# A decode step and its gradients on one core: the zero runs of two outputs lengthened by parking a softmax tile in DRAM, and a weight pass in whole row blocks

## The chip, the core and the metric

The kernel runs on 1 core of one Trainium2 chip. The metric is device time in microseconds of one execution, and a result is the median over several runs. A core has TensorE (PE, with its weight loads shown as PEld), VectorE (DVE), ScalarE (ACT), GpSimd (POOL) and SyncE (SP), which all work beside each other, and 16 DMA engines, which move data between DRAM and the core's on-chip memory. In this kernel SP issues nearly all transfers, in program order, on one queue.

## The reference, cut to what matters

Two layers, A (attention of one token over a sliding window of the cache) and B (a two-matrix MLP with the mish activation), are applied twice: A1, B2, A3, B4. Both rounds use the same weights. The result is the output and the gradients of it with respect to the input, both caches and all weights.

```python
def _A_ref(x, k_cache, v_cache, wq, wo):
    W = min(4096, max(256, Sk // 4))                 # 4096 of Sk = 32768
    q = heads(x @ wq)                                # 32 heads of 128, 4 key/value heads
    k = repeat(k_cache[:, :, Sk - W:, :], 8); v = repeat(v_cache[:, :, Sk - W:, :], 8)
    p = softmax((q @ k.T) * (Dh ** -0.5))
    return merge(p @ v) @ wo                         # wq: 1024 x 4096, wo: 4096 x 1024
def _B_ref(x, w1, b1, w2):
    h = x @ w1 + b1                                  # w1: 1024 x 3584, w2: 3584 x 1024
    return (h * tanh(softplus(h))) @ w2
def _f(x, ...):
    x = x + _A_ref(_layernorm(x), ...); x = x + _B_ref(_layernorm(x), ...)
    x = x + _A_ref(_layernorm(x), ...); x = x + _B_ref(_layernorm(x), ...)
    return x
out, vjp = jax.vjp(_f, ...); grads = vjp(grad_out)
```

All data is bf16. Only the last 4,096 of 32,768 cache rows take part, so 28,672 rows of each of the 4 heads of both cache gradients (out_2 and out_3) are zero: 58.7 MB of zeros, which the kernel writes from a zeroed tile.

## The kernel before, in words

One token is a matrix-vector problem, so the kernel is a long chain of small steps, and beside it the weights are read (several times, since they don't all fit), the zeros are written, and at the end the weight gradients, outer products of the kept vectors, are written out.

The chain in order: `attn_fwd` A1, `mlp_B2_fwd`, `attn_fwd` A3, `mlp_B4` (forward and backward of the last layer in one pass over w1), `ln_bwd`, `attn_bwd` A3, `mlp_B2_bwd`, `attn_bwd` A1, and a list of output jobs (`run_jobs`) that starts inside the last `attn_bwd` through `out_step`.

**Tiles.** Large tiles stay in fixed places for the whole kernel: `wq`, `wo`, `K`, `V` and `misc`. `misc` has 128 partitions x 4,096 bf16, cut into four quarters of 1,024 columns (2 KB): `sB` (0), `sA` (1), `zlo` (2), `sC` (3). `sC` holds the softmax rows p of A1 from the first attention to the last step; `sB` holds those of A3, `sA` the score gradients ds of A3. Before A3, the first two quarters (`misc[:, 0:2048]`) also serve as slot 0 of the ring `r2`. `zlo` is always zero; `zt` (quarters 1 and 2) is zero from the end of `mlp_B2_fwd` until A3's ds is written.

**Zeros.** `zero_jobs` holds 112 units, 14 per head and output; a unit is 2,048 columns on 128 partitions, 512 KB. `zeros(n)` issues n units on SP, up to four adjoining ones in one transfer. The source `zsrc` is a zeroed tile and its width: it is repeated over the destination by a broadcast, so the width sets the length of the contiguous run that one packet moves. The calls of `zeros` with their counts are written by hand into the stages. Until the end of `mlp_B2_fwd` the width is 1,024 columns (2 KB, `zlo`), then 2,048 (4 KB, `zt`) until the last block of B4's w1 pass, then 1,024 again, and from `out_step(0)` on 4,096 (8 KB, a part of `wo`).

**Weight loads.** `queue` is a list of loads in fixed order. `pump()` (L172) issues the first entries on SP as long as their slots are free; `rel(ring, i)` gives a slot back and pumps. The rings are `r2` (6 slots, w1 and w2 of the forward pass), `r4` (w1 blocks of B4), `rb` (w2 of the backward pass, slots of 2,048 columns of `K`) and `r8` (w1 of the backward pass, 8 slots of 1,792 columns of `K`). `r8` lies on the memory of `rb`: a slot of `rb` that no further w2 chunk needs becomes one or two slots of `r8` (L209). At the end the K heads are loaded again over `r8` (`K8`).

**The last w1 pass** (end of `mlp_B2_bwd`). w1's 8 row blocks of 128 rows are read as 16 halves of 128 x 1,792 (`w1h`). For each half TensorE turns 8 blocks, ACT copies them back over the half (`T8`, L235), VectorE does a multiply and sum over 768 columns (`ttr`, L593), and one half later `pairs` multiplies the turned blocks and releases the half's slot.

**Order.** The schedule is written by hand: SP works through its transfers in program order, and each waits for its data, its destination, and a free completion semaphore. SP uses eight of these in turn, so that in the trace a transfer is issued only once the one eight places earlier has landed.

Of the kernel before, what the change touches and what calls it, by code (L numbers as in the profile page):

```python
# [9 lines left out]
BF16 = mybir.dt.bfloat16  # L10
# [11 lines left out]
def kernel(  # L22
# [41 lines left out]
    ctx.enter_context(tc.manual_schedule())  # L64
    keep = ctx.enter_context(tc.tile_pool(name="keep", bufs=1))
    pt = ctx.enter_context(tc.tile_pool(name="pt", bufs=3, space=bass.MemoryType.PSUM))
    pone = ctx.enter_context(tc.tile_pool(name="pone", bufs=1, space=bass.MemoryType.PSUM))

    nc.scalar.preload_act_table_set("natural_log_exp_and_others")
# [14 lines left out]
    kp = kt([P, TJ, P], BF16, "kp")  # L84
    jk = kt([P, WC], BF16, "jk")
    misc = kt([P, 4096], BF16, "misc")
    sB, sA, zlo, zt, sC = misc[:, 0:1024], misc[:, 1024:2048], misc[:, 2048:3072], misc[:, 1024:3072], misc[:, 3072:4096]
    Kf = K[:].rearrange("p g t d -> p g (t d)")
    Kl = K[:].rearrange("p g t d -> p (g t d)")
    Vf = V[:].rearrange("p g t d -> p g (t d)")  # L90
# [47 lines left out]
    def zeros(n, after=None):  # L138
        while n > 0 and zero_jobs:
            zf, i = zero_jobs.pop(0)  # L140
            k = 1
            while k < min(n, 4) and zero_jobs and zero_jobs[0][1] == i + k:
                zero_jobs.pop(0)
                k += 1
            dst, run = zf[:, i * 2048:(i + k) * 2048], zsrc[1] if k * 2048 % zsrc[1] == 0 else 2048
            if run < k * 2048:
                d = nc.sync.dma_start(dst.rearrange("p (a b) -> p a b", b=run), zsrc[0][:, None, :].to_broadcast([P, k * 2048 // run, run]))
            else:
                d = nc.sync.dma_start(dst, zsrc[0][:, 0:run])
            gate(d, after)  # L150
            after = None
            n -= k
# [4 lines left out]
    slots = dict(r2=[misc[:, 0:2048]] + [wo[:, 20 + 2 * i:22 + 2 * i, :].rearrange("p h d -> p (h d)") for i in range(1, 6)],  # L157
                 r4=[Kl[:, 2048 * i:2048 * (i + 1)] for i in range(4, 8)])
    slots["rb"] = [Kl[:, 2048 * i:2048 * (i + 1)] for i in range(8)]
    slots["r8"] = [Kl[:, 2048 + F // 2 * i:2048 + F // 2 * (i + 1)] for i in range(8)]  # L160

    def w_view(w, key):
        if key[0] == "w2":
            return w.rearrange("p (t d) -> p t d", t=2), w2_v[key[1]]
        if key[0] == "w1h":
            t, hf = key[1] // 2, key[1] % 2
            w = w[:, 0:F // 2]
            return w, w1_v[:, t, hf * (F // 2):(hf + 1) * (F // 2)]
        b, i = key[1], key[2]
        nt = 2 if b < 3 else 4  # L170
        return w.rearrange("p (t f) -> p t f", t=nt), w1_v[:, nt * i:nt * i + nt, b * 1024:b * 1024 + 2048 // nt]

    def pump():
        while queue:
            it = queue[0]
            if it[0] == "w":
                fr = rings[it[1]]
                if not fr:
                    return
                i = fr.pop(0)  # L180
                v, src = w_view(slots[it[1]][i], it[2])
                nc.sync.dma_start(v, src)
                held[it[2]] = (v, it[1], i)
            elif it[0] == "K":
                fr = rings[it[1]]
                if len(fr) < 2:
                    return
                assert (fr.pop(0), fr.pop(0)) == (2 * it[2] - 4, 2 * it[2] - 3)
                nc.sync.dma_start(K[:, it[2], :, :], k_v[:, it[2]])
            elif it[0] == "K8":  # L190
                if rings["r8"][0:2 * it[1] + 2] != list(range(2 * it[1] + 2)):
                    return
# [12 lines left out]
            queue.pop(0)  # L205

    def rel(ring, i):
        if ring == "rb" and not any(it[0:2] == ("w", "rb") for it in queue):
            rings["r8"] += [6, 7] if i == 7 else [i - 1]  # L209
        else:  # L210
            rings[ring].append(i)
        pump()

    def take(key):
        return held.pop(key)
# [4 lines left out]
    queue += [("wo", s) for s in ([2, 3], [4, 5], [1])]  # L220
    queue += [("w", "r4", ("w1b", b, i)) for b in range(4) for i in range(4 if b < 3 else 2)]
    queue += [("K", "r4", g) for g in (3, 2)]
    queue += [("w", "rb", ("w2", c)) for c in range(NW2)] + [("w", "r8", ("w1h", i)) for i in range(16)]
    queue += [("K8", g) for g in range(G)]

# [232 lines left out]
    def attn_fwd(x_col, l, first, p_dst, F_, Z_):  # L459
        sv, n_bf, g0 = ln_fwd(x_col, l)  # L460
        if first:
            constants()
        zeros(Z_[0])
        big = two_banks()
        for t in range(TD):
            for n in range(8):
# [65 lines left out]
                    unit("V", Vf[:, g, u * 1024:(u + 1) * 1024])  # L532
        for h in range(2):
            nc.scalar.activation(p_dst[:, h * 512:(h + 1) * 512], big[h][:], ACT.Exp, bias=nb[:, 0:1], scale=-1.0)
        o_bf = opair[:, LI[l], :]
        go = nc.vector.tensor_copy(o_bf, acc[:])
        pps = sm_tile(P, HQ)
# [101 lines left out]
            nc.vector.tensor_mul(d3[:, 1, :], dps[:], m3[:, 1, :])  # L639

    def mlp_B2_fwd(x_col):
        zeros(4)
        sv, n_bf, g0 = ln_fwd(x_col, "B2")
        hacc = one_tile("acc", TF)
# [14 lines left out]
        mish(h, apair[:, 1, :], dact[:], TF, jkf)  # L659
        sv["dact"] = dact  # L660
        R, dps, ds = w2_pass(apair[:, 1, :], gpair[:, LI["B4"], :], {8: 1, 9: 1, 10: 1, 11: 1})
        nc.gpsimd.memset(sA, 0.0)
        make_identity(nc, ident_f)
        zsrc[:] = [zt, 2048]
        da4 = kt([P, TF], FP32, "da4")
        y = d_cols(R)
        x_new = kt([P, TD], FP32, "x_B2")
# [4 lines left out]
    def mlp_B4(x_col, da4):  # L672
# [64 lines left out]
        for b in range(4):  # L737
            fwd(b)
            fill(FB4[b][0])
            sel(b)  # L740
            act(b)
            turn(b, 0, 8 if b < 3 else 4)
            fill(FB4[b][1])
            bwd(b)
            if b == 3:
                zeros(2)
                zsrc[:] = [zlo, 1024]
            zeros(ZB4[b] - 2 * (b == 3))
        evac(jkf[:, 0:256], R[:, 0:256], 256, "D")
        dn = sm_tile(P, TD)  # L750
        for i in range(2):
# [68 lines left out]
    def mlp_B2_bwd(g_col, g_bf, sv, x3):  # L820
        bcast_g(g_bf)
        R, dps, ds = w2_pass(apair[:, 0, :], g_bf, {10: 1})
        zeros(3)
        dh = kt([P, TF], FP32, "dh_B2")
        da_merge(dh[:], dps, ds, sv["dact"][:])
        nc.vector.tensor_copy(hpair[:, 1, :], dh[:])
# [19 lines left out]
        def pairs(i, w, ring, sl):  # L846
            t, hf = i // 2, i % 2
            for k in range(8):
                fb = hf * NW2 + k
                mm(nacc[:, t:t + 1], w[:, k * P:(k + 1) * P], hpair[:, 1, fb:fb + 1], i == 0 and k == 0, hf == 1 and k == 7)  # L850
            rel(ring, sl)
            zeros({9: 2, 12: 1, 14: 1}.get(i, 0))

        for i in range(16):
            w, ring, sl = take(("w1h", i))
            T8([w[:, (k // 2) * 256 + k % 2:(k // 2) * 256 + k % 2 + 255:2] for k in range(8)], w[:, 0:1024], "A")
            ttr(w[:, 1024:1792], dhb[i % 2][:, 0:768], nv[:, i:i + 1])
            if pend:
                pairs(*pend.pop())
            pend.append((i, w, ring, sl))  # L860
# [311 lines left out]
```

## Time and profile before

| | |
|---|---|
| median of 3 runs | 426.61 us (425.5 to 426.96) |
| profiled execution, its own time | 426.93 us |
| its span, first to last instruction | 425.1 us |
| mean granted TensorE clock | 0.764 |
| TensorE, VectorE, ScalarE, GpSimd busy | 317.7, 234.5, 220.1, 13.8 us |
| DRAM read, written | 70.27 MB, 98.58 MB (397 GB/s over the span) |
| DMA packets | 43,990, 169.44 MB; 37,036 under 8 KB |

How to read it: times are microseconds. Line numbers (L182) are those of the kernel below; L142 to L149 are the zeros, L182 the weight loads from the rings, L204 other loads from `queue`, L966 to L1102 the outputs. "out<-in" names the tiles an instruction writes and reads. An arrow behind an idle time names what ended it. A stretch's DMA share is the time that packets started in it took, over 16 engines; it can be a little over 1, as packets overlap. A DMA's landing is the time at which its completion is signalled.

| from | to (about) | stage |
|---|---|---|
| 0 | 65 us | A1 forward: wq, K, V, wo loaded |
| 65 | 109 us | B2 forward: w1 and w2 in ring `r2` |
| 109 | 145 us | A3 forward |
| 145 | 218 us | B4 forward and backward, w1 in ring `r4` |
| 218 | 247 us | A3 backward |
| 247 | 292 us | B2 backward: w2 in `rb`, then w1 in `r8` |
| 292 | 310 us | A1 backward |
| 310 | 425 us | output jobs |

### The profile page before, as it was taken

To read this page: it belongs to the slowest core of one execution; us is meant where nothing else is said; L and a number is where in the kernel's file an instruction comes from. 1 tells how busy PE (TensorE), PEld (TensorE's weight loads), DVE (VectorE), ACT (ScalarE), POOL (GpSimd) and SP (SyncE) were. 2 spreads that over 40 slices of the span, in tenths; PEclk is the share of its full clock that TensorE was granted. 3 is DMA by queue.
4 is the path that set the end of the run, shared out by engine and by line. 5 is a ranking of instruction groups with operands and counts; after the bars stand their busy time and mean duration, and the time that the engine had idled before them with its cause. 6 is when DMAs were issued, how large, how long until landed. Compare 5 with 4: busy or idle time off the path is not lost.

```text
span 425.1 us, 9110 instructions
## 1 busy us (share of the span) xinstructions
PE 317.7 (75%) x3768; PEld 189.1 (44%) x3768; DVE 234.5 (55%) x532; ACT 220.1 (52%) x335; POOL 13.8 (3%) x56
## 2 busy tenths in 40 slices
PE   2477736368697887878889888787699899979830
PEld 1155315346456575766756556764323223322100
DVE  2035102069445453655647279684467999889940
ACT  1035101037345364556554247493577899889950
POOL 2000000000000000000000000000400100030000
PEclk9999655559799898999989969698955555555555
DMA  8999999999999999999999999999999999999996
GB/s 326 424 421 419 424 411 407 412 410 374 390 413 407 419 417 373 420 374 407 339 420 406 341 408 406 388 368 406 416 421 421 421 422 417 415 406 389 400 420 263
DMA packets 43990, 169.44 MB, mean 399 GB/s; under 512 B 3088, under 2 KB 4140, under 8 KB 37036
## 3 DMA queue, kind: packets, MB, share of 16 engines
q1 hardware_dynamic: 43792, 168.83, 99.4%
q8 instruction: 29, 0.48, 0.4%
q14 instruction: 13, 0.11, 0.1%
q0 software_dynamic: 96, 0.01, 0.0%
q10 hardware_dynamic: 60, 0.01, 0.0%
HBM read 70.27 MB, written 98.58 MB: 397 GB/s over the span
## 4 chain that ended last, share of the span: by engine, by line
PE 27%; ACT 9%; DMA 6%; DVE 6%; issue 2%; POOL 0%; ACTq 0%; POOLq 0%; SPq 0%; DVEq 0%
DMA K<-in_B_w_dram 6%; PE R L242 5%; PE op L242 5%; PE tp L262 3%; PE acc L242 3%; PE sm L242 3%; ACT K L235 3%; ACT V L896 2%; PE lo L242 2%; PE hi L242 2%; ACT wo L896 2%; PE tp L927 2%; DVE jk L233 1%; DVE K L893 1%; ACT wq L896 1%
## 5 line engine op out<-in xcount | busy, mean ns | idle before, releaser
L235 ACT COPY K<-tp 128x1024 bf16<-128x1024 bf16 x54 | 52.8, 1016 | 10.6 <-PE tp L262 9.0
L262 PE MATMUL tp<-ident_bf,K 128*128 128x128 bf16 x656 | 50.0, 232 | 5.8 <-ACT K L235 3.1
L242 PE MATMUL op<-wo 2*128 2x512 bf16 (+2 forms) x115 | 47.2, 563 | 4.3 <-ACT wo L896 1.2
L262 PEld LDWEIGHTS <-K 128*128 128x128 bf16 x656 | 42.3, 105 | 12.9 <-issue 10.4
L242 PEld LDWEIGHTS <-wo 2*128 2x128 bf16 (+1 forms) x510 | 21.0, 103 | 47.5 <-issue 39.5
L235 ACT COPY wo<-tp 128x1024 bf16<-128x1024 bf16 x27 | 27.4, 1026 | 26.2 <-PE tp L262 23.6
L593 DVE CUSTOM_DVE_ANT_0 K<-K,kp 128x1024 bf16<-128x1024 bf16 (+1 forms) x22 | 24.7, 1127 | 3.4 <-PE R L242 1.4
L262 PE MATMUL tp<-ident_bf,wo 128*128 128x128 bf16 x336 | 25.4, 231 | 0.6 <-ACT wo L235 0.5
L233 DVE COPY jk<-R 128x512 f32<-128x512 f32 (+1 forms) x11 | 7.3, 665 | 32.8 <-PE R L242 32.8
L242 PE MATMUL lo<-wo 2*128 2x512 bf16 x41 | 24.4, 594 | 0.0
L242 PE MATMUL hi<-wo 2*128 2x512 bf16 x41 | 24.4, 594 | 0.0
L262 PEld LDWEIGHTS <-wo 128*128 128x128 bf16 x336 | 21.0, 104 | 7.5 <-issue 7.4
L235 ACT CAST jk<-hi 128x512 bf16<-128x512 f32 x4 | 3.8, 946 | 35.6 <-PE hi L242 35.6
L233 DVE CAST jk<-lo 128x512 bf16<-128x512 f32 x4 | 4.0, 996 | 30.5 <-PE lo L242 30.5
L233 DVE COPY K<-tp 128x1024 bf16<-128x1024 bf16 x22 | 14.9, 689 | 9.4 <-PE tp L262 9.3
L233 DVE COPY wo<-tp 128x1024 bf16<-128x1024 bf16 x19 | 12.8, 688 | 12.4 <-PE tp L262 12.3
L242 PE MATMUL acc<-wo 2*128 2x512 bf16 (+1 forms) x33 | 19.6, 594 | 0.0
L235 ACT COPY wq<-tp 128x1024 bf16<-128x1024 bf16 x13 | 13.0, 1018 | 11.8 <-PE tp L262 7.9
L242 PEld LDWEIGHTS <-npair 128*32 128x32 bf16 x184 | 6.4, 117 | 27.0 <-issue 23.5
L896 ACT CAST wo<-op 128x512 bf16<-128x512 f32 (+1 forms) x28 | 17.1, 623 | 1.2 <-PE hi L242 1.1
L361 ACT ACTIVATE cols<-cols,eps_t 128x1 f32<-128x1 f32 x4 | 1.2, 294 | 31.8 <-DVE cols L358 31.8
L262 PE MATMUL tp<-ident_bf,wq 128*128 128x128 bf16 x240 | 16.2, 219 | 1.6 <-ACT K L235 0.6
(310 smaller groups left out, 710.2 us busy)
## 6 DMA issues: line engine op xcount, KB each, us to landing
out_dram<-misc SPq DMA_DIRECT2D x15, 2048.0 KB, 19.7
K<-in_B_w_dram SPq DMA_DIRECT2D x28, 512.0 KB, 8.3
wo<-in_A_wo_dram SPq DMA_DIRECT2D x10, 1024.0 KB, 19.9
K<-in_A_k_cache_dram SPq DMA_DIRECT2D x9, 1024.0 KB, 10.6
wq<-in_A_wq_dram SPq DMA_DIRECT2D x8, 1024.0 KB, 10.0
out_dram<-wq SPq DMA_DIRECT2D x8, 1024.0 KB, 12.0
out_dram<-misc SPq DMA_DIRECT2D x7, 1024.0 KB, 12.8
K<-in_B_w_dram SPq DMA_DIRECT2D x16, 448.0 KB, 6.2
```

What stands on the lines that cost most here:

```text
L233: return nc.vector.tensor_copy(out_ap, in_ap)
L235: return nc.scalar.copy(out_ap, in_ap)
L242: return nc.tensor.matmul(out_ap, lhsT=lhsT, rhs=rhs, start=start, stop=stop, skip_group_check=True, **kw)
L262: nc.tensor.transpose(ps[:, b * P:(b + 1) * P], ap, ident_bf[:])
L361: nc.scalar.activation(lnv[:], var[:], ACT.Ln, bias=eps_t[:, 0:1], scale=1.0)
L593: return nc.vector.tensor_tensor_reduce(out=w, in0=w, in1=vec, scale=1.0, scalar=0.0, op0=ALU.mult, op1=ALU.add, accum_out=acc_col)
L893: nc.vector.tensor_copy(out_ap, in_ap)
L896: nc.scalar.copy(out_ap, in_ap)
L927: nc.tensor.transpose(ps[:, j * P:(j + 1) * P], spread_t[:, j, :], ident_bf[:])
```

## The change

p of A1 is stored to a DRAM tile `p1_d` (256 KB) right after it is computed, and its place `sC` is zeroed by GpSimd. `sC` is loaded again in the last w1 pass, after half 11. In between `sC` is a source of zeros, and `zsrc` is:

- from `mlp_B2_fwd` on `misc[:, 2048:4096]`, 2,048 columns (was 1,024);
- after w2's forward pass all of `misc`, 4,096 columns, for A3's first 8 units (was 2,048); for this GpSimd zeroes `misc[:, 0:2048]` (was `sA` alone);
- then `misc[:, 1024:4096]`, 3,072 columns (6 KB), to the end of B4's third block (was 2,048);
- then `misc[:, 2048:4096]` up to `zeros(3)` in `mlp_B2_bwd` (was 2,048 for two units, then 1,024), then `zlo` as before.

`zeros` now joins up to six adjoining units, and takes only as many as the run's width divides. The w1 pass of `mlp_B2_bwd` reads whole row blocks, 8 transfers of 128 x 3,584 (runs of 7,168 B) into 4 slots of `r8`, instead of 16 halves into 8 slots. A slot is released after its second half, and the `rb` slots 2, 4, 6 and 7 release the four of `r8`. The arithmetic on the halves is unchanged.

```diff
+    dram = ctx.enter_context(tc.tile_pool(name="dram", bufs=1, space=bass.MemoryType.DRAM))
-    sB, sA, zlo, zt, sC = misc[:, 0:1024], misc[:, 1024:2048], misc[:, 2048:3072], misc[:, 1024:3072], misc[:, 3072:4096]
+    sB, sA, zlo, sC = misc[:, 0:1024], misc[:, 1024:2048], misc[:, 2048:3072], misc[:, 3072:4096]
+    p1_d = dram.tile([P, WC], BF16, name="p1_d")
...
-            while k < min(n, 4) and zero_jobs and zero_jobs[0][1] == i + k:
-                zero_jobs.pop(0)
+            while k < min(n, 6) and k < len(zero_jobs) + 1 and zero_jobs[k - 1][1] == i + k:
                 k += 1
+            per_src = {4096: 2, 3072: 3}.get(zsrc[1], 1)
+            k -= k % per_src if k > per_src else 0
+            del zero_jobs[0:k - 1]
...
-    slots["r8"] = [Kl[:, 2048 + F // 2 * i:2048 + F // 2 * (i + 1)] for i in range(8)]
+    slots["r8"] = [Kl[:, 2048 + F * i:2048 + F * (i + 1)] for i in range(4)]
...
+        if key[0] == "w1f":
+            return w, w1_v[:, key[1], :]
...
-                if rings["r8"][0:2 * it[1] + 2] != list(range(2 * it[1] + 2)):
+                if rings["r8"][0:it[1] + 1] != list(range(it[1] + 1)):
...
-            rings["r8"] += [6, 7] if i == 7 else [i - 1]
+            rings["r8"] += {2: [0], 4: [1], 6: [2], 7: [3]}.get(i, [])
...
-    queue += [("w", "rb", ("w2", c)) for c in range(NW2)] + [("w", "r8", ("w1h", i)) for i in range(16)]
+    queue += [("w", "rb", ("w2", c)) for c in range(NW2)] + [("w", "r8", ("w1f", t)) for t in range(TD)]
...
         zeros(Z_[0])
+        if not first:
+            zsrc[:] = [misc[:, 1024:4096], 3072]
...
+        if first:
+            nc.sync.dma_start(p1_d[:], p_dst)
+            nc.gpsimd.memset(sC, 0.0)
...
     def mlp_B2_fwd(x_col):
+        zsrc[:] = [misc[:, 2048:4096], 2048]
         zeros(4)
...
-        nc.gpsimd.memset(sA, 0.0)
+        nc.gpsimd.memset(misc[:, 0:2048], 0.0)
         make_identity(nc, ident_f)
-        zsrc[:] = [zt, 2048]
+        zsrc[:] = [misc[:], 4096]
...
             if b == 3:
-                zeros(2)
-                zsrc[:] = [zlo, 1024]
-            zeros(ZB4[b] - 2 * (b == 3))
+                zsrc[:] = [misc[:, 2048:4096], 2048]
+            zeros(ZB4[b])
...
         zeros(3)
+        zsrc[:] = [zlo, 1024]
...
-            rel(ring, sl)
+            if hf:
+                rel(ring, sl)
+            if i == 11:
+                nc.sync.dma_start(sC, p1_d[:])
             zeros({9: 2, 12: 1, 14: 1}.get(i, 0))
...
-            w, ring, sl = take(("w1h", i))
+            if i % 2 == 0:
+                full, ring, sl = take(("w1f", i // 2))
+            w = full[:, i % 2 * (F // 2):(i % 2 + 1) * (F // 2)]
```

More of the change, by code (lines that the diff above doesn't have):

```diff
@@ L141, in zeros @@
             k = 1
-            while k < min(n, 4) and zero_jobs and zero_jobs[0][1] == i + k:
-                zero_jobs.pop(0)
+            while k < min(n, 6) and k < len(zero_jobs) + 1 and zero_jobs[k - 1][1] == i + k:
                 k += 1
+            per_src = {4096: 2, 3072: 3}.get(zsrc[1], 1)
+            k -= k % per_src if k > per_src else 0
+            del zero_jobs[0:k - 1]
             dst, run = zf[:, i * 2048:(i + k) * 2048], zsrc[1] if k * 2048 % zsrc[1] == 0 else 2048
             if run < k * 2048:
-                d = nc.sync.dma_start(dst.rearrange("p (a b) -> p a b", b=run), zsrc[0][:, None, :].to_broadcast([P, k * 2048 // run, run]))
+                d = nc.sync.dma_start(dst.rearrange("p (a b) -> p a b", b=run), zsrc[0][:, None, 0:run].to_broadcast([P, k * 2048 // run, run]))
             else:
```

## Prediction

> **What bounds the kernel now.** The first view is the page's busy time and its DMA rows, to see which resource is full.
>
> ```profile
> PE 317.7 (75%) x3768; PEld 189.1 (44%) x3768; DVE 234.5 (55%) x532; ACT 220.1 (52%) x335; POOL 13.8 (3%) x56
> DMA  8999999999999999999999999999999999999996
> q1 hardware_dynamic: 43792, 168.83, 99.4%
> ```
>
> No compute engine is over 75%, while the DMA engines are busy in every slice: the packets of SP's queue took 99.4% of 16 engines' span. Second view, the busy time by stretch, over stretches in which packets of one size dominate (columns: stretch, length, the five engines, PE clock, DMA share, GB/s).
>
> ```profile
> 26.00:60.00 34.00, 23.95 (x282) 15.73 (x281) 10.70 (x23) 10.80 (x16) 0.00 (x0) 0.76 1.01 420
> 78.00:86.00 8.00, 3.72 (x98) 3.15 (x98) 0.00 (x0) 0.00 (x0) 0.00 (x0) 0.50 1.02 410
> 141.00:157.00 16.00, 13.45 (x194) 10.29 (x182) 8.33 (x30) 8.30 (x11) 0.00 (x0) 0.89 1.02 418
> 228.00:236.00 8.00, 6.82 (x114) 4.65 (x115) 5.11 (x10) 3.10 (x4) 0.19 (x1) 1.00 1.05 405
> ```
>
> In that order: 8 KB loads, 3.5 KB w1 loads, 4 KB zeros, 2 KB zeros. All are full; only the rate differs, by the run. The trace's packet records give the price of one: median 84 ns at 2,048 B, 140 at 3,584, 159 at 4,096, 272 at 7,168, 309 at 8,192. All lie on 9 ns + bytes/27.3 per ns; 6,144 B, which the trace lacks, comes to 234 ns by that line (estimate, between the rows of 4 and 8 KB). Third view, TensorE's timeline, for what the rate does to compute.
>
> ```profile
> 79.38 0.53 PE L242 MATMUL acc<-npair,wo 128*128 128x1 bf16 x14 [0.66 <-DMA wo<-in_B_w_dram]
> 80.46 0.53 PE L242 MATMUL acc<-npair,wo 128*128 128x1 bf16 x14 [0.55 <-DMA wo<-in_B_w_dram]
> 81.59 0.53 PE L242 MATMUL acc<-npair,wo 128*128 128x1 bf16 x14 [0.60 <-DMA wo<-in_B_w_dram]
> 82.72 0.53 PE L242 MATMUL acc<-npair,wo 128*128 128x1 bf16 x14 [0.60 <-DMA wo<-in_B_w_dram]
> ```
>
> A half row block of w1 comes every 1.12 us: its 128 packets over 16 engines are 8 x 140 ns = 1.12 us, nothing else. So I read SP's queue as one stream: transfers land one behind the other, spaced by (packets / 16) x (time of one). Added up so, from the first landing (5.58 us) to the last of the four wo outputs issued at 408 to 411 us, the 185 transfers explain all but about 12 us of the span, and most of what is left is single steps of 0.4 to 1.3 us in landings. I found no wait of SP that empties the stream. Its longest waits end with enough still queued: the w1 loads issued from 123.87 us land from 132.68, the w2 load issued at 250.88 lands at 257.82, behind 2 MB of zeros.
>
> A transfer needs some lead. The first one, with nothing ahead, was issued at 0.74 and landed at 5.58 us, 2.47 us of it data, so 2.4 us are overhead. A transfer issued at least 2.4 us before its predecessor lands leaves no hole. The tightest leads now are 3.95 us (wq output issued at 389.76, predecessor landed at 393.71), 4.0 (w2 load at 101.19, predecessor at 105.17) and about 4.7 (w1 load at 275.74).
>
> **The change, part by part.** A unit of zeros is 512 KB. At 2, 4, 6 and 8 KB it costs 1.344, 1.272, 1.248 and 1.236 us.
>
> Zeros. I followed every call of `zeros` in both versions. Before: 8,960 packets of 2 KB, 8,064 of 4 KB, 896 of 8 KB, which is 144.48 us of the stream. After: 2,048 of 2 KB, 4,736 of 4 KB, 3,840 of 6 KB, 1,408 of 8 KB: 141.17 us. Gain 3.31 us: 27 units go from 2 to 4 KB (1.94), 45 from 4 to 6 KB (1.08), 8 from 4 to 8 KB (0.29). The units and their places stay; three transfers fewer are issued, at 0.4 to 0.7 us of SP each, which SP's waits hide.
>
> Last w1 pass. 2,048 packets of 3,584 B (17.92 us) become 1,024 of 7,168 B (17.41 us): gain 0.51 us, and eight issues fewer.
>
> p1's round trip. 256 KB out and 256 KB back are 128 packets of 2 KB each way, at 84 ns: 0.67 us each, loss 1.34 us. A copy into a DRAM tile that is read back has no row. The nearest are the 2 KB zeros (0.67 us for 128 packets) and the 2 KB w1 loads of B4, 256 packets each, which landed 1.29 to 2.08 us apart, so 0.65 to 1.04 us for 128. I take the zeros' value, which is also what most of those loads show, and keep 1.3 to 2.1 us for both ways together.
>
> Sum on the stream: -3.31 - 0.51 + 1.34 = -2.48 us.
>
> What is queued behind each new wait. The store of p1 waits for ACT's second Exp (44.08 + 0.68 us) and stands ahead of the first w1 load, now issued at 46.79. As SP reuses a completion semaphore only when the transfer eight places earlier has landed, that load moves one place, to 49.3 us; with 15 us of wo still in the stream this costs nothing. p1 lands right behind the last wo block (64.23 us), at about 64.9. GpSimd's memset of sC waits for that and takes 0.95 us (its row for the same size at 103.74), so the first four zeros are issued at about 66.2 instead of 61.77 us. Their predecessor lands at 71.5: lead 5.3, no hole. GpSimd has nothing else to do until 103. The memset of 2,048 columns takes about 1.9 us there instead of 0.95; its reader, `zeros(8)`, is issued at 111.48. That `zeros(8)` now reads sB, which A3's Exp overwrites at 134.63 us; the transfers land at about 131, 3.6 us of cover; were they late, ACT would wait for the difference. The reload of sC is queued behind the second K block at about 287 us, lands near 294, and is needed at 302.9: 9 us of cover. sA, written at 230.91, is read by fewer late zeros than before.
>
> The coarser slots of w1. Block 0 waits for two w2 chunks instead of one (261.53 instead of 259.56 us); its predecessor lands at 265.47, lead 3.9. Block 4 waits for both halves of block 0 (276.64 instead of 275.74): lead about 2.4 to 3 us after the gains ahead of it, the tightest place of the new kernel. A hole of 0 to 0.6 us is possible. And the last block lands whole, so two halves are turned after it instead of one: one ACT copy more, 1.02 us, on the compute chain.
>
> How compute follows. Running total of the stream, after minus before: +0.67 after p1, +0.24 when w2's chunks land (98 us), -0.8 at the loads of B4's block 1 (165), -1.3 at block 3 (208), -2.4 at w2's chunk 7 (258), -3.2 at the last w1 block, -2.5 after p1's reload. In each of these places TensorE waits for the load today (2.5 us at 165.08, 1.3 at 186.79, 1.0 at 208.03, 0.7 at 257.86), so compute moves up with the stream; behind the w1 pass it is -3.2 + 1.02 = about -2.1 us. In the output stage compute is then 0.4 us less advanced than the stream, and the lead of 3.95 us at 389 shrinks to 3.5: still no hole. The end is the stream's, -2.48 us.
>
> Against the time: the profiled execution took 426.93 us (span 425.1 and 1.8 around it), 0.3 above the median of the runs, 426.61. 426.61 - 2.48 = 424.1 us, 0.58% faster. Some 0.3% is what a measurement of this kernel can tell from no change.
>
> The Trainium skill, "DMA: Bandwidth & Descriptors", section "Why small descriptors are slow (HBM only)", gives a fixed cost of about 3 cycles per packet. At the 850 MHz of its section "Where 436 GB/s comes from" that is 3.5 ns, and the sum would be about -0.2 us (an estimate from that page of the Trainium skill); the records here show 9 ns.
>
> **The rivals.**
>
> 1. A packet's fixed cost is smaller in throughput than in its own record. In the 2 KB stretch the share is 1.05: packets overlap. By the rates (405, 418, 420 GB/s) 27 units gain 0.04 us each, the other 53 about 0.3 together, the w1 pass 0.43, and p1 costs 1.3: net -0.5 us, 426.1. For it: the GB/s rows. Against: the landings, which go by whole packet times.
>
> 2. Slower: longer runs gain nothing, since what a packet waits for is bytes alone; then only p1's 0.5 MB stays, +1.34 us, 428.0 us. It decides from a fixed cost per packet under 3 ns (6,900 packets x 3 / 16 = 1.3 us). For it: 7 KB, 8 KB and 4 KB lie within 1% in GB/s. Against: the 2 KB stretch, 405 GB/s beside 418 at 4 KB. The Trainium skill, "DMA: Bandwidth & Descriptors", section "Specifications", puts the minimum transfer for line rate at 512 B, which speaks for this rival; by that rule all runs here are long enough, and the two stretches disagree with it.
>
> 3. The w1 pass runs dry. If blocks 4 to 7 come each 0.5 us too late for the stream, 2 us go: -0.5 us, 426.1. For it: the lead of 2.4 us; against: the four slots give a cycle of 2.2 us per block, and ACT's 2.04 us per block keeps ahead of that.
>
> **How the numbers follow.** Forecast 0.66; rival 1 0.12; rival 2 (with any stall behind p1's store) 0.11; rival 3 0.11. Rivals 1 and 3 fall mostly within 0.3% (425.3 to 427.9), and a tenth of the forecast does too, as its gain is only twice that bound: faster 0.64, same 0.24, slower 0.12. The range starts at 422.8, where mean packet times (87.2 ns at 2 KB, 162 at 4 KB, 147.8 and 277 in the w1 pass) take the place of the medians and the net gain becomes about 3.7 us, and ends at 426.7, which takes in rivals 1 and 3. The forecast's own range is 423.3 to 425.0.
>
> **What would show it.** The zeros of B4 as 6,144 B packets at about 234 ns; some 6,650 packets fewer on SP's queue and 0.5 MB more; the same share near 99%. TensorE's wait at 165.08 shorter by 0.8 us or earlier by as much; the last w1 matmul near 289 instead of 291.4; the last four outputs issued 2 us earlier. It is wrong if the DMA share drops below 0.9 at 66 to 72 us or at 276 to 286 us, if ACT waits at its A3 Exp for a transfer, or if 6 KB packets take over 243 ns, 1.5 times the 4 KB row's 159 plus the noise of 4 ns.

## The result: slower by 0.43%

The changed kernel takes 428.11 us (median of 12 runs) beside 426.35 us of the kernel before (12 runs): ratio 1.0043, 95% interval 1.0023 to 1.0064. It is slower, where 0.58% faster was forecast, and the time lies outside the range. In a second series, with the experiments, it was 428.09 beside 426.33 (1.0034, 1.0013 to 1.0056). The profile shown here is of that second series (429.6 us, the slowest of its 12 executions, span 427.8), because the first execution profiled ran at a clock of .56 throughout, unlike the others. Sizes read from it are therefore on the high side.

The page after, busy time and DMA rows:

```profile
PE 320.5 (75%) x3768; PEld 191.1 (45%) x3768; DVE 233.9 (55%) x532; ACT 220.0 (51%) x335; POOL 15.7 (4%) x57
DMA  8999999999999999999999799999999999998998
q1 hardware_dynamic: 36992, 169.36, 98.5%
```

SP's queue has 6,800 packets fewer (forecast: some 6,650) and 0.5 MB more, as forecast; its share fell from 99.4 to 98.5%, and there are slices with less than 9 tenths in the middle and at the end. The packets have the forecast prices: median 234 ns at 6,144 B, 272 at 7,168, 159 at 4,096, 84 at 2,048. So the stream became cheaper, and the kernel slower. Busy time by stretch after (columns as before: stretch, length, five engines, PE clock, DMA share, GB/s); the first four are those of the prediction:

```profile
26.00:60.00 34.00, 24.25 (x283) 15.60 (x282) 10.70 (x23) 10.72 (x16) 0.00 (x0) 0.75 1.01 420
78.00:86.00 8.00, 3.76 (x101) 3.16 (x98) 0.00 (x0) 0.00 (x0) 0.00 (x0) 0.50 1.03 410
141.00:157.00 16.00, 14.01 (x190) 9.99 (x190) 7.64 (x29) 7.66 (x11) 0.00 (x0) 0.89 1.02 423
228.00:236.00 8.00, 6.82 (x120) 5.22 (x120) 6.16 (x13) 3.75 (x5) 0.26 (x1) 1.00 1.02 415
...
190.00:210.00 20.00, 15.37 (x236) 12.95 (x236) 10.50 (x29) 11.67 (x13) 0.00 (x0) 1.00 0.97 374
256.00:270.00 14.00, 11.66 (x189) 8.61 (x186) 11.76 (x22) 9.10 (x10) 0.00 (x0) 0.94 0.99 365
270.00:283.00 13.00, 10.02 (x134) 8.63 (x134) 8.31 (x19) 8.67 (x10) 0.00 (x0) 0.76 1.02 412
283.00:296.00 13.00, 10.19 (x137) 8.70 (x138) 7.88 (x19) 8.10 (x8) 0.00 (x0) 0.50 0.95 350
```

and the last four stretches in the kernel before:

```profile
190.00:210.00 20.00, 15.95 (x246) 13.28 (x246) 11.29 (x30) 11.97 (x14) 0.00 (x0) 1.00 0.98 371
256.00:270.00 14.00, 10.71 (x177) 7.79 (x174) 11.43 (x22) 8.94 (x9) 0.00 (x0) 0.97 1.02 389
270.00:283.00 13.00, 11.61 (x158) 10.19 (x159) 9.51 (x22) 9.38 (x11) 0.00 (x0) 0.77 1.02 382
283.00:296.00 13.00, 9.90 (x148) 6.32 (x149) 7.96 (x22) 7.38 (x8) 0.00 (x0) 0.89 1.03 402
```

The zeros of B4 (141 to 157 us) run at 423 instead of 418 GB/s, those at 228 us at 415 instead of 405. What is lost stands in the last w1 pass, 283 to 296 us: 350 GB/s instead of 402 (0.68 MB, 1.6 us at 418 GB/s), the granted clock .50 instead of .89. There TensorE's timeline after shows the place (the first two lines are the earlier w1 pass, paced by its loads at about 1.1 us per half, as before):

```profile
79.84 0.54 PE L248 MATMUL acc<-npair,wo 128*128 128x1 bf16 x14 [0.58 <-DMA wo<-in_B_w_dram]
80.99 0.54 PE L248 MATMUL acc<-npair,wo 128*128 128x1 bf16 x14 [0.61 <-DMA wo<-in_B_w_dram]
...
280.81 0.35 PE L248 MATMUL acc<-hpair,K 128*128 128x1 bf16 x8 [0.24 <-ACT K L241]
283.55 1.03 PE L268 MATMUL tp<-ident_bf,K 128*128 128x128 bf16 x8 [2.39 <-DMA K<-in_B_w_dram]
284.38 0.39 PE L248 MATMUL acc<-hpair,K 128*128 128x1 bf16 x8
284.63 1.01 PE L268 MATMUL tp<-ident_bf,K 128*128 128x128 bf16 x8
```

and in the kernel before:

```profile
280.50 0.61 PE L262 MATMUL tp<-ident_bf,K 128*128 128x128 bf16 x8
281.34 0.35 PE L242 MATMUL acc<-hpair,K 128*128 128x1 bf16 x8 [0.23 <-ACT K L235]
281.58 0.62 PE L262 MATMUL tp<-ident_bf,K 128*128 128x128 bf16 x8
282.25 0.35 PE L242 MATMUL acc<-hpair,K 128*128 128x1 bf16 x8
```

Before, TensorE goes from half 7 to half 8 (block 4's first) without a stop, though with nothing to spare: half 8 landed at 281.54 us, 0.04 us ahead of its turn. After, it waits 2.39 us for the whole of block 4, which lands at 283.50, and then turns a half in 1.01 us instead of 0.61. ScalarE's timeline after, at the end of the pass and at the first cast of A1's backward:

```profile
292.82 2.09 ACT L241 COPY K<-tp 128x1024 bf16<-128x1024 bf16 x2 [1.25 <-PE tp L268]
...
303.62 1.30 ACT L241 CAST jk<-hi 128x512 bf16<-128x512 f32 x1 [8.70 <-PE hi L248]
```

and before:

```profile
285.58 5.44 ACT L235 COPY K<-tp 128x1024 bf16<-128x1024 bf16 x5
...
298.56 1.30 ACT L235 CAST jk<-hi 128x512 bf16<-128x512 f32 x1 [7.53 <-PE hi L242]
```

In these two profiles the last copy of the pass ends at 294.91 instead of 291.03 us (+3.9), the cast starts 5.1 us later. Compute keeps that: the issue of the V output moves from 395.17 to 399.98 us (+4.8), the last outputs' from 408.39 to 413.20. The span grows by only 2.7 us, because the last outputs waited 8.0 us in the queue before (issued 408.39, first landed 416.35) and 6.1 after.

### The profile page after: what moved, and what is told of

It is laid out like the page before. It is cut to its first block, busy times and chain, and to the rows that moved or that the text cites. A ratio compares the mean times of both kernels' runs of the same rounds, so it can differ in the third digit from the quotient of the medians.

```text
span 472.1 us, 9093 instructions
## 1 busy us (share of the span) xinstructions
PE 386.5 (82%) x3768; PEld 238.2 (50%) x3768; DVE 236.2 (50%) x532; ACT 221.9 (47%) x335; POOL 15.8 (3%) x57
## 4 chain that ended last, share of the span: by engine, by line
PE 60%; DMA 20%; ACT 7%; DVE 7%; issue 1%; POOL 0%; ACTq 0%; SPq 0%; POOLq 0%; DVEq 0%
PE tp L268 23%; PE R L248 11%; PE sm L248 6%; PE acc L248 5%; PE op L248 5%; DMA V<-in_A_v_cache_dram 4%; DMA wo<-in_B_w_dram 4%; PE lo L248 4%; DMA wo<-in_A_wo_dram 4%; PE hi L248 4%; DMA wq<-in_A_wq_dram 3%; DMA K<-in_B_w_dram 3%; ACT V L913 2%; ACT wo L913 2%; PE tp L944 1%
## 5 line engine op out<-in xcount | busy, mean ns | idle before, releaser
L268 PE MATMUL tp<-ident_bf,K 128*128 128x128 bf16 x656 | 69.0, 289 | 3.3 <-DMA K<-in_B_w_dram 2.0
L268 PEld LDWEIGHTS <-K 128*128 128x128 bf16 x656 | 59.1, 130 | 10.9 <-issue 6.6
L268 PE MATMUL tp<-ident_bf,wo 128*128 128x128 bf16 x336 | 34.4, 283 | 0.0
L268 PEld LDWEIGHTS <-wo 128*128 128x128 bf16 x336 | 28.4, 124 | 8.4 <-issue 7.6
L268 PE MATMUL tp<-ident_bf,wq 128*128 128x128 bf16 x240 | 24.3, 282 | 0.0
L268 PEld LDWEIGHTS <-wq 128*128 128x128 bf16 x240 | 21.3, 127 | 3.8 <-issue 3.0
L248 PEld LDWEIGHTS <-misc 32*128 32x128 bf16 (+1 forms) x154 | 7.9, 102 | 22.0 <-issue 15.7
L248 PE MATMUL R<-wo,operm 128*32 128x512 bf16 x128 | 13.9, 594 | 5.7 <-DMA wo<-in_A_wo_dram 5.4
```

What stands on the lines that cost most here:

```text
L248: return nc.tensor.matmul(out_ap, lhsT=lhsT, rhs=rhs, start=start, stop=stop, skip_group_check=True, **kw)
L268: nc.tensor.transpose(ps[:, b * P:(b + 1) * P], ap, ident_bf[:])
```

## Experiments

Theory at the start: the row blocks lose the time, through coarse slots. Rivals: the round trip or the zeros lose it. Each kernel's ratio is to runs of the kernel before on the same chip (medians 426.28 to 426.49).

| kernel | median us | ratio [95%] |
|---|---|---|
| changed kernel | 428.09 | 1.0034 [1.0013, 1.0056] |
| without the trip | 427.21 | 1.0017 [0.9997, 1.0037] |
| halves | 426.65 | 1.0006 [0.9984, 1.0028] |
| row blocks alone | 428.81 | 1.0040 [1.0010, 1.0071] |
| trip alone | 427.77 | 1.0023 [1.0002, 1.0045] |
| longer zeros alone | 425.77 | 0.9975 [0.9953, 0.9998] |
| shorter zeros | 428.34 | 1.0043 [1.0020, 1.0067] |
| half 7 earlier | 427.45 | 1.0033 [1.0009, 1.0056] |
| transposes before half 8 | 428.24 | 1.0054 [1.0030, 1.0079] |
| zeros behind the blocks | 429.37 | 1.0068 [1.0041, 1.0096] |
| row blocks, zeros behind, half 7 earlier | 429.03 | 1.0067 [1.0047, 1.0087] |
| before, zeros behind | 429.19 | 1.0051 [1.0022, 1.0080] |
| blocks 0 to 3 whole | 426.26 | 1.0001 [0.9977, 1.0024] |
| blocks 4 to 7 whole | 426.95 | 1.0028 [1.0008, 1.0048] |
| halves, transposes before chunk 7 | 426.46 | 1.0015 [0.9990, 1.0040] |
| transposes at both places | 428.31 | 1.0048 [1.0023, 1.0072] |
| blocks 0 to 3 whole, hole filled | 426.67 | 1.0014 [0.9996, 1.0032] |
| before, hole filled | 426.56 | 1.0019 [1.0000, 1.0039] |

### The three parts

The changed kernel again:

> The changed kernel itself, for its trace and its distance to the kernel before on one chip. Three theories. T1, the coarse w1 blocks: the stream of transfers runs dry in the last w1 pass, and one more ACT copy follows the last block; then the trace has a hole in the landings there of 3 us or more, and the stages ahead of it are 2 to 3 us earlier than in the kernel before. T2, packets cost bytes alone: no new hole anywhere, but the stages are never ahead of the kernel before, and p's round trip adds 1.3 us. T3, compute doesn't follow: the stream is ahead of the kernel before, but holes open in front of the loads of B4 and of the backward w2 pass, because their slots are released no earlier. All three: about +1.8 us.

The changed kernel without the round trip (p of A1 is lost, its place holds zeros, so A1's ds is not the reference's):

```diff
-            nc.sync.dma_start(p1_d[:], p_dst)
-                nc.sync.dma_start(sC, p1_d[:])
```

> The changed kernel without p1's store and reload (p of A1 is lost, so the last score gradients and the v gradient of A1 are computed from zeros); zero runs and w1 blocks as changed. T1: the hole in the w1 pass stays, only the 1.34 us of the round trip go: about +0.5 us against before. T2: everything that costs is gone: 0.0 us. T3: the stream has more slack still, holes grow by as much: +1 to +1.8 us.

The changed kernel with the w1 pass back in 16 halves and 8 slots:

```diff
-    slots["r8"] = [Kl[:, 2048 + F * i:2048 + F * (i + 1)] for i in range(4)]
+    slots["r8"] = [Kl[:, 2048 + F // 2 * i:2048 + F // 2 * (i + 1)] for i in range(8)]
...
-            rings["r8"] += {2: [0], 4: [1], 6: [2], 7: [3]}.get(i, [])
+            rings["r8"] += [6, 7] if i == 7 else [i - 1]
...
-            if hf:
-                rel(ring, sl)
+            rel(ring, sl)
```

> The changed kernel with the last w1 pass back in 16 halves and 8 slots; zero runs and round trip as changed. T1: the loss is gone and the gain of the zeros is left, -2.0 us against before. T2: +1.3 us. T3: +1 to +1.8 us.

The kernel before with the row blocks alone (that edit the other way round):

```diff
-            rings["r8"] += [6, 7] if i == 7 else [i - 1]
+            rings["r8"] += {2: [0], 4: [1], 6: [2], 7: [3]}.get(i, [])
```

> The kernel before with the w1 row blocks alone (4 slots, 8 transfers); zeros and p1 as before. T1: +2 us or more. T2: 0.0 us. T3: 0 to +0.5 us. By the packet prices of the prediction alone: -0.5 us on the stream, +1.0 us on the chain.

The kernel before with the round trip alone:

```diff
+            nc.sync.dma_start(p1_d[:], p_dst)
+            nc.gpsimd.memset(sC, 0.0)
...
+            if i == 11:
+                nc.sync.dma_start(sC, p1_d[:])
```

> The kernel before with p1's store and reload and the memset of sC alone; zeros and w1 pass as before. If the stream of transfers is the bound everywhere: +1.3 us, its 256 packets of 2 KB. If the stream has holes that take it up: 0 to +0.5 us.

The changed kernel with halves and without the round trip: the longer zero runs alone (p of A1 lost as above; the edits of both kernels above):

```diff
-                nc.sync.dma_start(sC, p1_d[:])
...
-            rings["r8"] += {2: [0], 4: [1], 6: [2], 7: [3]}.get(i, [])
+            rings["r8"] += [6, 7] if i == 7 else [i - 1]
```

> The kernel before with the longer zero runs alone: no round trip (p of A1 is lost, so the last score gradients and the v gradient of A1 are computed from zeros), w1 in 16 halves. Prediction's packet prices: -3.3 us against before. Rival 1 of the prediction, by the GB/s rows: -1.3 us. Rival 2, bytes alone: 0.0 us.

By the ratios, the parts measured alone come to 1.7 us for the row blocks, 1.0 for the trip and -1.1 for the longer zeros, together 1.6 beside 1.4 for the whole change. As differences of medians on one chip, the row blocks cost 1.4 us (changed kernel less halves) and the trip 0.9 (changed kernel less the one without it). The intervals are wide: 0.4 to 3.0 us for the row blocks alone, 0.1 to 1.9 for the trip, 0.1 to 2.0 for the gain of the zeros. The row blocks are the main loss. The trip costs about what the stream sum gave it. The zeros bring a quarter to a third of the 3.31 us of the sum, which lies outside their interval. So taking the row blocks out doesn't give the forecast back: the kernel with halves stands at +0.3 us where theory one expected -2.0, as the longer zeros only pay for the trip.

Theory one is right about the place and not about its signs. The loss in the last w1 pass is there, but the stretch loses 1.6 us and not 3, and the stages ahead of it are not 2 to 3 us earlier: by 256 us the stream of the profile after has moved as many bytes as before, to 0.03 MB.

### How much a run length is worth

The kernel before with its 4 KB zeros in runs of 2 KB. The expectation counted 55 units; it is 63, which makes its figures 4.5 us by packets and 2.3 by rates.

```diff
-        zsrc[:] = [zt, 2048]
```

> The kernel before with the 55 units of zeros that it writes in 4 KB runs put back to 2 KB runs (the narrow source is kept), a change of run length with nothing else beside it. Packet prices: 55 x 0.072 = +4.0 us. GB/s rows: 55 x 0.037 = +2.0 us. Bytes alone: 0.0 us.

Measured: +1.85 us by the medians (0.9 to 2.9 by the interval of the ratio). The 2 KB zeros at 141 us run at 405 GB/s (4 KB: 418; 6 KB: 423), which is the size by the rates, not by the packets. But the stretch with B4's last block shows something else too:

```profile
190.00:210.00 20.00, 15.15 (x236) 12.86 (x233) 11.13 (x30) 11.89 (x13) 0.00 (x0) 1.00 1.05 389
```

Here the kernel before has 371 GB/s and a share of .98: with a slower stream a hole of the DMA engines at 200 to 204 us is gone. In the packet records of before they are busy 89% at 200 to 202 us and 60% at 202 to 204. So part of the extra packets filled time that was empty. A stream with holes is not the only limit, and holes grow when it gets shorter. The stretches of the kernel with the longer zeros alone:

```profile
240.00:256.00 16.00, 11.83 (x167) 8.09 (x167) 10.88 (x23) 7.67 (x8) 0.00 (x0) 0.89 1.01 402
256.00:270.00 14.00, 11.80 (x153) 9.09 (x151) 10.02 (x20) 7.45 (x8) 0.00 (x0) 0.74 0.92 333
```

and its TensorE:

```profile
255.03 0.40 PE L246 MATMUL R<-K,apair 128*32 128x512 bf16 x4 [2.54 <-DMA K<-in_B_w_dram]
255.36 0.62 PE L266 MATMUL tp<-ident_bf,K 128*128 128x128 bf16 x8
255.81 0.35 PE L246 MATMUL acc<-gpair,K 128*128 128x1 bf16 x8
256.27 0.62 PE L246 MATMUL R<-K,apair 128*32 128x512 bf16 x4
256.82 1.03 PE L266 MATMUL tp<-ident_bf,K 128*128 128x128 bf16 x8
```

By 256 us this stream has moved 1.6 MB (3.8 us) more than before: the packet sum's gain is there. In the next 14 us it moves 333 GB/s, the kernel before 389, and half of the lead is gone (1.9 us at 270). TensorE waited 2.54 us for w2's chunk 7 (before: 0.61), then took 1.7 us a chunk at the lower clock, and its slots came back slower than loads landed.

### The last w1 pass

Half 7's products ahead of half 8's transposes, so that block 7's slot is given back before the wait for block 4:

```diff
             pend.append((i, w, ring, sl))
+            if i == 7:
+                pairs(*pend.pop())
```

> The changed kernel with one step moved: the products of half 7 are done at once, and no longer after TensorE has turned half 8, for which it waits until row block 4 has landed. If the row blocks lose their time because block 7's load is issued only after block 4 has landed (284.85 us in the trace of the changed kernel), block 7's load is issued 2 us earlier or more, lands right behind block 6, and the kernel is about 1.5 us faster than the changed one, +0.2 us against before. If the loss is elsewhere (the whole block before its first half can be used, or the load itself): no change, +1.5 us.

Block 7's load is issued at 282.30 instead of 284.85 us, and the wait for block 7 (0.80 us in the changed kernel) is gone. TensorE's stop ahead of block 4 is now two, of 0.57 and 0.74 us with half 7's products between them, and block 4 is turned from 282.96 instead of 283.55 us. The clock still falls to .50, and the time is 427.45, within the noise of the changed kernel: the gain of 1.5 us in the expectation is not there.

To part the lower clock from the lateness, 32 transposes into a tile that nobody reads, ahead of half 8:

```diff
+            if i == 8:
+                idle = ptile()
+                for b in range(32):
+                    nc.tensor.transpose(idle[:, b % 8 * P:(b % 8 + 1) * P], wq[:, 0, b * P:(b + 1) * P], ident_bf[:])
```

> The changed kernel with 32 transposes of wq into an unread PSUM tile in front of the transposes of half 8 (block 4's first), so TensorE works through most of its wait for block 4; loads, copies and results stay. Theory one, the 2.4 us without work is what drops the granted clock: TensorE's longest wait there falls under 0.8 us, the clock of 283 to 296 us is .8 or more instead of .50, the eight transposes of a half take 0.62 us and not 1.01, and the time is 0.6 to 1.4 us under the changed kernel's (426.7 to 427.5). Theory two, only the lateness of the blocks costs: the clock may rise, but the last copy of the pass still ends at 294 to 295 us and the time stays at 428.0. Theory three, the clock there falls for a reason other than the wait: .50 remains, 428.0 to 428.5.

```profile
282.26 1.95 PE L876 MATMUL tp<-ident_bf,wq 128*128 128x128 bf16 x32
284.75 0.62 PE L268 MATMUL tp<-ident_bf,K 128*128 128x128 bf16 x8 [0.54 <-DMA K<-in_B_w_dram]
285.20 0.34 PE L248 MATMUL acc<-hpair,K 128*128 128x1 bf16 x8
285.41 0.61 PE L268 MATMUL tp<-ident_bf,K 128*128 128x128 bf16 x8
...
289.09 1.04 PE L268 MATMUL tp<-ident_bf,K 128*128 128x128 bf16 x8
```

The halves take 0.62 us again (until 289 us, mean clock of 283 to 296 us .73), but the last copy ends at 295.67 and the time is 428.24. That is theory two, the lateness and not the clock, with a reserve. From block 4 on TensorE turned a block in 2.2 us at the full clock and in 2.4 at the low one, and in both profiles it then waited for block 7 (0.82 and 0.80 us), whose load is issued late (284.85 us in the changed kernel): that wait takes up what the clock gives. A kernel with both steps, half 7 earlier and the transposes, was not run.

Then the 3 zero units that stand ahead of the blocks, moved behind half 9: in the changed kernel, in the kernel before with row blocks (with half 7 earlier too), and in the kernel before:

```diff
-        zeros(3)
...
-            zeros({9: 2, 12: 1, 14: 1}.get(i, 0))
+            zeros({9: 5, 12: 1, 14: 1}.get(i, 0))
```

> The changed kernel with the 3 zero units that it issues ahead of the w1 pass moved behind the row block loads (5 units instead of 2 after half 9, at 2 KB; same bytes). If block 4 is late because those 1.5 MB stand ahead of it: it lands by about 280.5 us instead of 283.5, TensorE's wait for it falls from 2.4 us to under 0.8, the clock of 283 to 296 us is .8 or more, the last copy of the pass ends at 290 to 291.5 us instead of 294.9, and the time is 1.3 us or more under the changed kernel's: 425.8 to 426.8. If the blocks' own size makes it late (slot given back too late), the wait stays over 1.5 us and the time at 427.5 to 428.5.

> The kernel before with the whole row blocks alone, the 3 zero units moved behind their loads, and half 7's products ahead of half 8's transposes, so that the last block's load is issued earlier. If the late block 4, the clock after it and the late last block are all that the rows cost, their +1.7 us is gone: 426.0 to 427.0, the last copy of the pass at 289.5 to 291 us. If the rows cost something else, 427.5 to 428.8.

> The kernel before with nothing but its 3 zero units ahead of the w1 pass moved behind half 9 (5 units there). Its own longest wait in that pass is 0.84 us (VectorE). If the order of the zeros matters only where a load is late: within 0.3% of before, 425.8 to 426.8. If the zeros' place itself brings or costs time, outside of that; by that sign the moves in the other two kernels are read.

All three are slower, by 2 to 3 us beside before, also the one without row blocks: my remedy was worse than the fault. In the changed kernel block 4 did land early, at 277.96 instead of 283.50, TensorE's longest wait in the pass fell from 2.39 to 1.22 us, and the last copy ended at 289.59; the clock of 283 to 296 us stayed at .50. But the stream ran empty. The kernel before with nothing else changed has

```profile
270.00:283.00 13.00, 11.76 (x157) 10.30 (x158) 9.84 (x22) 9.00 (x11) 0.00 (x0) 0.79 0.80 300
```

where it had 382 GB/s: 1.07 MB, 2.5 us. What is queued behind comes later: the second K head lands at 299.94 instead of 295.88 us. The zeros there are not in the way of the blocks only; they are what the stream lives on while no slot is free.

Which blocks lose: the kernel with halves, with blocks 0 to 3 read whole into two neighbouring half slots and 4 to 7 as halves, and then the other way round.

```diff
-    queue += [("w", "rb", ("w2", c)) for c in range(NW2)] + [("w", "r8", ("w1h", i)) for i in range(16)]
+    queue += [("w", "rb", ("w2", c)) for c in range(NW2)] + [("w", "r8", ("w1f", t)) for t in range(4)] + [("w", "r8", ("w1h", i)) for i in range(8, 16)]
```

> The changed kernel with blocks 0 to 3 of the last w1 pass read whole and blocks 4 to 7 as halves, each half in a slot of its own, given back on its own. Theory one, the loss is made where a block's load waits for two halves to be given back: it stands with the kernel that has halves throughout, 426.3 to 427.0, the DMA share of 283 to 296 us at 1.02, not .95. Theory two, whole rows cost wherever they are: half of the 1.5 us or more stays, 427.3 to 428.0.

```diff
+    queue += [("w", "rb", ("w2", c)) for c in range(NW2)] + [("w", "r8", ("w1h", i)) for i in range(8)] + [("w", "r8", ("w1f", t)) for t in range(4, 8)]
```

> The other way round: blocks 0 to 3 as halves, blocks 4 to 7 whole, each in the two slots of a pair of halves. Theory one: all of the loss, 427.7 to 428.5, the DMA share of 283 to 296 us under .98. Theory two: 427.0 to 427.6.

With blocks 4 to 7 as halves the loss is gone, ratio 1.0001; in 283 to 296 us it is the stretch of before again:

```profile
283.00:296.00 13.00, 9.83 (x145) 6.45 (x146) 8.02 (x22) 7.44 (x8) 0.00 (x0) 0.82 1.03 405
```

With blocks 4 to 7 whole most of it is there, ratio 1.0028 (the median, 426.95, is less than theory one expected; the two intervals overlap). The sign in its profile failed: the share of 283 to 296 us is not under .98, and the stretch ahead of it is low instead:

```profile
270.00:283.00 13.00, 10.64 (x161) 9.09 (x160) 9.57 (x23) 10.22 (x12) 0.00 (x0) 0.76 0.95 358
283.00:296.00 13.00, 10.53 (x133) 7.71 (x135) 6.74 (x20) 6.32 (x7) 0.00 (x0) 0.50 1.03 404
```

TensorE waits only 0.88 us for block 4 there, and that execution took 425.67 us. The profile of the row blocks alone has the longest wait for block 4, 3.57 us, in an execution of 426.31. So the times show that whole blocks 4 to 7 cost; how much of it each wait makes, single profiles do not show.

A wait for two slots alone is not the cause: blocks 0 to 3 have it too, for the slots of two w2 chunks (the first is issued at 261.00 us instead of 259.56 before), and they cost nothing that the times show. The difference in the traces is the time in hand. Before, halves 4 and 5 landed 4.5 us or more ahead of their turn on TensorE, and block 3 read whole still landed 2.1 us ahead of its own (276.79 and 278.91 us); halves 8 and 9 landed 0.04 us ahead of theirs.

### Is it the clock, or the holes?

24 transposes ahead of chunk 7 in the second w2 pass, with halves, and in the changed kernel with the 32 ahead of half 8:

```diff
+            if c == 7 and 10 in Z_ and 8 not in Z_:
+                idle = ptile()
+                for b in range(24):
+                    nc.tensor.transpose(idle[:, b % 8 * P:(b % 8 + 1) * P], wq[:, 0, b * P:(b + 1) * P], ident_bf[:])
```

> The changed kernel with halves in the last w1 pass (426.65 before) and 24 transposes of wq into an unread PSUM tile, 1.9 us, ahead of chunk 7 of the second w2 pass, where TensorE waits 1.7 us for its load. If the clock that falls after that wait makes the holes: the transposes of a chunk take 0.62 us instead of 1.03 at 256 to 260 us, the time with fewer than 16 packets in flight at 256 to 270 us falls from 1.1 us to under 0.5, and the time is 0.4 to 1.4 us less, 425.2 to 426.2. If the lateness alone makes them: 426.4 to 427.0, holes as before. The transposes themselves can cost up to 0.3 us where the wait is shorter.

> The changed kernel with the 24 transposes ahead of w2's chunk 7 and the 32 ahead of half 8. The 32 alone brought nothing (428.24). If the clock after chunk 7's wait counts: 426.7 to 427.7; if not: 427.9 to 428.6.

The first profile has a clock of 1.00 at 256 to 270 us (halves alone: .77) and a share of 1.00 instead of .94, and 426.46 us beside 426.65; the second is at 428.31. Neither moved the time beyond the noise. In the first, though, the stream was level with before at 210 us and not 2 us ahead as with halves alone, so its profile does not show the wait that the transposes were to cover; whether the clock costs the zeros some of their gain is bounded by the times alone.

One zero unit moved ahead of B4's block 3, into the hole at 200 us:

```diff
-    ZB4 = [12, 11, 9, 7]
+    ZB4 = [12, 11, 10, 6]
```

> The changed kernel with halves for blocks 4 to 7 (426.26) and one zero unit more ahead of the load of B4's block 3, one less behind it. If the stream sets the time and the holes are its loss: time with fewer than 16 packets in flight at 165 to 210 us falls by 1 us or more from 3.25, and the time by 0.4 to 1.2 us: 425.1 to 425.9. If the hole is only time in which compute is the limit, the load of block 3 lands later, TensorE waits for it by as much more, and nothing is gained: 426.0 to 427.3.

> The kernel before with the same one unit moved (11, 10, 6 instead of 11, 9, 7). Its hole is 1.2 us. If the stream sets the time: the hole under 0.4 us and 425.4 to 426.2. If compute is the limit there: TensorE's wait for block 3 grows from 1.0 us by up to 1.2, and the time stays at 426.3 or rises to 427.

Nothing gained, 426.67 and 426.56. The unit did not even close the hole:

```profile
190.00:210.00 20.00, 17.36 (x267) 14.72 (x264) 12.46 (x33) 12.19 (x14) 0.00 (x0) 1.00 0.95 357
```

is the stretch of the kernel before with the unit moved (371 GB/s without). In that profile the stream was 1.0 us ahead at 210 us and 2.9 at 283, and its hole then came at 283 to 296 us: 351 GB/s. There the hole only moved. That it goes to wherever the stream next gets ahead of the slots is a reading of these profiles, not a test.

## The prediction, step by step

Right: the packet counts and prices; p1's round trip (1.34 us forecast, 0.9 to 1.3 measured, with an interval of 0.1 to 1.9); what is queued behind p1's store (it landed at 64.80 us, forecast 64.9; the first w1 load 0.5 us later than before).

Between the forecast of -2.5 us and the measured +1.8 lie 4.2 us. Two terms of the sum make them, each about half: the row blocks, -0.51 us in the sum and +1.4 to +1.7 measured, and the zeros, -3.31 us in the sum and -0.7 to -1.1 measured. None of the signs of being wrong that the prediction named for the stream and its packets showed (DMA share 1.03 at 66 to 72 us and 1.01 at 276 to 286 us, 6 KB packets 234 ns): in that profile block 4 came late in a full stream.

Wrong:

- **"The coarser slots of w1".** I allowed block 4 a hole of 0 to 0.6 us and the end of the pass one ACT copy, 1.02 us. TensorE waited 2.39 us there (3.57 in the profile of the row blocks alone), and the last copy ended 3.9 us late. I compared the issue of a load with the landing of its predecessor, so I asked whether the *stream* has a hole. I did not ask when TensorE needs the block: it has turned half 7 at 280.6 us, and before, half 8's load needed only 0.46 MB to land. A whole block makes it wait for 0.92 MB behind the same zeros. Rival 3 had the place, and with its 2 us also about the size (-0.51 + 2 is +1.5 us for the row blocks); it ended at 426.1 because it kept the 3.31 us of the zeros. Its reason, a stream that runs dry by 0.5 us a block, is not what made block 4 late.
- **"Last w1 pass: gain 0.51 us".** Absent. By medians a packet costs 272 instead of 2 x 140 ns, but the mean in this pass is 305 ns beside 2 x 153.
- **"How compute follows" and "the end is the stream's".** I let the waiting compute move up by what the stream gained, to -2.1 us behind the w1 pass. In the changed kernel it was +3.9 there. With the longer zeros alone the stream was 3.8 us ahead at 256 us and the time gained 0.7. What lies behind is **"I found no wait of SP that empties the stream"**: the trace of before has the stretch of 371 GB/s at 190 to 210 us, where block 3's load is issued at 201.67 us after the zeros ahead of it are through. I judged by leads at the tightest loads and by the page's DMA row, where a 9 can hide 1 us in each slice of 10.6 us. My reading is that stream and slots limit the kernel in turn, and that a gain of the one is partly lost to the other; no run shows this by itself.
- **Rival 1** has the zeros' size: the rates give 27 x 0.04 + 45 x 0.015 (418 to 423 GB/s), about 1.8 us; measured 0.7 to 1.1, with 1.8 still inside the interval. Whether the rest is lost in holes alone, or packets that overlap never gave it, is not settled: moving one zero unit into a hole brought nothing, and the stream's place at one time differs by 1 to 3 us between profiles of kernels that are alike up to there.
- **Rival 2**, slower, gave 428.0 and came true in the time only: longer runs do gain (0.9975 alone), and its loss was to be p1's bytes, which are well under half of the real one. The rule of the Trainium skill that stood behind it (512 B is enough for line rate; "DMA: Bandwidth & Descriptors", "Specifications") is not borne out: 405, 418 and 423 GB/s at 2, 4 and 6 KB.

Not settled: how block 4's wait divides between its late issue and its size. It landed 2.1 us after the zeros ahead of it (281.40 and 283.50 us), so its first half alone would have been there about 1.05 us sooner (estimate, half of that); the other 1.3 us of the wait are open. The kernel with half 7 earlier treats block 7 only. Of the steps tried, only reading blocks 4 to 7 in halves again won the loss back.

## What to carry to other kernels

When several small loads become one, ask when the consumer needs the *first* piece and when the last piece's slot comes free, not only whether the queue has a hole: here reading blocks whole cost nothing where they still landed 2 us ahead of their turn, and 1.4 us where the halves before had landed just in time. Where a queue is busy 99% of the time, look for stretches of 2 us below that before you call it the bound; if there are any, price a gain of the queue at a fraction. Filler transfers ahead of a critical load can be what keeps the queue busy: moving three zero units cost 2.2 to 2.7 us.

## What the runs showed of the hardware

- TensorE's clock halves with less idle time than I thought. In the changed kernel the granted clock fell to .50 at 282.0 us, 0.85 us into the wait of 2.39 us, and did not come back up to 296 us (0.62 to 1.01 us for eight transposes), though TensorE was busy three quarters of the time from 283 us on. It fell at this place in runs with shorter stops too: at 281.0 us with a stop of 0.88 us (blocks 4 to 7 whole), at 282.5 with stops of 0.57 and 0.74 (half 7 earlier), and with the 32 transposes at 289.1 with no stop over 0.54 us since 280. In the 3.4 us ahead of these four drops TensorE was busy for 2.0 to 2.4 us. The Trainium skill, "TensorE: Matmul & The Clock Gate", "Part 1: The HAM clock gate", puts the drop behind an idle window of about 3.4 us; none of these four drops had one.
- The lower clock cost nothing that the times show (428.24 us with the transposes that held it up until 289 us, 428.09 without): in both profiles TensorE then waits for block 7.
- So here the drop marks a stretch in which TensorE was short of work, not one long wait. It was the easiest sign of this loss to see, and holding the clock up did not cure it.
